# Running the mixer layers on two segments at once, with split norms and streamed mixer weights, in a fused recurrent-attention kernel

## The chip, the cores and the metric

One core of a Trainium2 chip. The metric is the device time of one execution in microseconds (us), lower is better; each figure is a median of several executions. All runs told here are of the undisturbed ("fast") state.

## The reference

Four layers on one sequence of 2048 tokens of width 640: A, B, A, B, each on the layer norm of its input and added to it. Reduced to what matters:

```python
def A(x):                         # x: 2048 x 640, seg 32, 32 heads of 192
    mem = mem0                    # 8 x 640
    for s in range(64):
        h = concat(mem, x[32*s : 32*s+32])          # 40 x 640
        q, k, v = h @ Wq, h @ Wk, h @ Wv            # each 640 -> 6144
        o = softmax(mask(q k^T / sqrt(192))) v @ Wo  # 6144 -> 640
        mem = o[:8]                                  # recurrent
        out[32*s : 32*s+32] = o[8:]

def B(x):
    n = layernorm(x)
    h = gelu(n @ w1)              # 640 -> 640; its quarters are shifted by
    x1 = x + shifted(h) @ w2      # -1, +1, -2, +2 tokens
    return x1 + gelu(layernorm(x1) @ w3) @ w4       # 640 -> 1536 -> 640

x = x + A(layernorm(x)); x = x + B(layernorm(x))    # and the same once more
```

The memory makes A a chain of 64 steps; a step has only 40 rows, but needs all of Wq, Wk, Wv and Wo, 31 MB in bf16, more than fits on the chip.

## The kernel before

Both A layers run in one loop. Iteration t works on segment t of the first A and on segment t - D_LAG of the second ("lanes"), 80 columns together. The heads go in eight groups of four. The weights of A are cut into 64 halves of 480 KB: 26 stay resident, 38 are streamed in each iteration through a ring of six buffers (`wst`) on the queue of SP. Layer B of the segments that A has just finished is cut into stages, one of which is issued at the end of each head group ("fillers"). Rows pass between layers through DRAM: `x1d` (after the first A), `x2d` (after the first B), `x3d` (after the second A).

```python
def a_main(t, hT, hT_n, pc, prep_next, fillers=()):
    cx = a_begin(t, hT, hT_n, pc)
    st_proj(cx, 0)                              # q, k, v of group 0
    if pending_xnew:
        a_xnew(pending_xnew.pop(0))             # x + A, stores to x1d and x3d (SP)
    pc_next = prep_next()                       # a_prep_load: loads of xs (SP) and their norms
    for g in range(NG):                         # NG = 8
        st_scores(cx, g)                        # pss
        if g + 1 < NG: st_proj(cx, g + 1)
        st_softmax(cx, g)                       # mx, nb (VectorE), exp (ScalarE), Pm
        if g >= 1: st_pt(cx, g - 1)             # transposes pst, eviction PT on ScalarE
        if g >= 2: st_wo(cx, g - 2)             # psy += Wo x oT
        if g >= 1: st_pv(cx, g - 1)             # pso, eviction oT on VectorE
        fillers[g]()                            # one stage of layer B
        ...

def s1a():                                      # layer B, first stage; 72 rows of two lanes
    ...
    nc.sync.dma_start(out=xw[...], in_=src[...])    # x1d / x3d
    layer_norm(xw, u, slice(0, XW))             # norm of x, then layer B's own norm of it:
    layer_norm(u, bv_c, slice(0, XW))           # bn_stats x2, bn_aggr, +eps (VectorE),
                                                # pow (GpSimd), apply (VectorE)
...
stages = [s1a, s1b, s1c, s2a, s2b, s2c(0, 6), s2c(6, 6), s3]   # s3 stores x2d and the output (SP)
```

An eviction here is the copy of a matmul's result from a PSUM tile to an SBUF tile. In the trace of this kernel VectorE reaches the eviction of oT only at 2038.65 us, behind the norms that it began at 2032.03. Likewise SP stands 3.74 us (from 2028.12) at the load of xs from `x2d`, until the store of x3d ahead of it has landed.

## Time and profile before

| | before |
|---|---|
| median of 6 runs | 4865.28 us (4852.06 to 4867.98) |
| TensorE busy, granted clock | 4025.0 us (83%), 0.917 |
| VectorE, ScalarE busy | 2805.0 us, 1994.9 us |
| DMA | 1355.8 MB, mean 279 GB/s |
| start, loop, end | 157 us to the second iteration, then 66 iterations of 69.2 us, 141 us from the last start to the end |

"Busy" is an average over the whole run. Where TensorE is busy 83% of the time, the question is what ends its idle time. The granted clock is the share of TensorE's full clock: in a stretch where it was 0.55, fifteen matmuls took 1.21 us instead of 0.70. The prediction shows the lines. In them PE is TensorE, PEld its weight loads, DVE VectorE, ACT ScalarE, POOL GpSimd, SP SyncE; a q behind a name is the engine's own sequencer, which issues DMAs; L297 is a line of the kernel. A line of waits reads: who waited for whom, us in total, times, longest. A row of windows reads: from:to and length in us, busy time (and instructions) of TensorE, weight loads, VectorE, ScalarE, GpSimd, then granted clock, DMA share, GB/s.

### The profile page before, as it was taken

The numbers are of one execution on the slowest core, as the hardware profiler recorded it, in microseconds if no ns is written. First come the engines' busy times: TensorE is split into PE (matmuls) and PEld (weight loads), VectorE is DVE, ScalarE is ACT, GpSimd is POOL, SyncE is SP. The second block draws the span as 40 slices with busy tenths as digits, with TensorE's granted clock in tenths as the row PEclk, the third lists the DMA queues.
The fourth block names the chain that finished last, engine by engine and source line by source line (L and its number), as shares of the span: only waits on it lengthen the run. The fifth ranks groups of instructions, "written<-read, shape, count | busy, mean of one in ns | idle before, by whom it ended". The sixth has DMA issues, their size and how long they took to land.

```text
span 4865.7 us, 174526 instructions
## 1 busy us (share of the span) xinstructions
PE 4025.0 (83%) x74804; PEld 3514.6 (72%) x74804; DVE 2805.0 (58%) x7270; ACT 1994.9 (41%) x7281; POOL 509.0 (10%) x1489
## 2 busy tenths in 40 slices
PE   1898888888988888889888888888889888988886
PEld 1777777777777777777777777777777777777774
DVE  1556555556565556555556565656565655555554
ACT  0444344434444444344434443444344434444442
POOL 1111110111011101110111011101110111011110
PEclk9999999999999999999999999999999999989997
DMA  9888778778887788778778887878788777877882
GB/s 370 306 289 287 267 282 284 281 267 286 292 282 271 281 285 283 266 276 284 279 260 290 283 284 271 285 278 285 269 286 291 280 266 281 293 274 274 287 293 98
DMA packets 437102, 1355.84 MB, mean 279 GB/s; under 512 B 51004, under 2 KB 91972, under 8 KB 436324
## 3 DMA queue, kind: packets, MB, share of 16 engines
q1 hardware_dynamic: 412724, 1320.43, 76.9%
q10 hardware_dynamic: 22368, 18.68, 1.1%
q8 instruction: 584, 9.57, 0.8%
q0 software_dynamic: 1232, 5.57, 0.3%
q14 instruction: 194, 1.59, 0.1%
HBM read 1326.13 MB, written 37.03 MB: 280 GB/s over the span
## 4 chain that ended last, share of the span: by engine, by line
PE 64%; DVE 16%; DMA 12%; POOL 3%; issue 3%; ACT 2%; SPq 0%; DVEq 0%; POOLq 0%; ACTq 0%
PE psv L441 13%; PE psy L548 10%; PE psq L403 10%; PE psk L403 9%; DMA xs<-in_A_x_dram 6%; DVE ln_st L293 5%; PE y2A L719 4%; POOL ln_rstd L296 3%; PE pss L483 3%; DMA wst<-wS 3%; PE hsA L684 3%; PE psh L709 2%; DVE oT L282 2%; PE pso L527 2%; PE pso L532 1%
## 5 line engine op out<-in xcount | busy, mean ns | idle before, releaser
L403 PEld LDWEIGHTS <-wst 128*128 128x128 bf16 x19380 | 824.4, 104 | 55.0 <-issue 28.4
L497 ACT ACTIVATE Pm<-pss,nb 80x80 bf16<-80x80 f32 x2176 | 679.4, 319 | 284.0 <-DVE nb L492 278.9
L441 PEld LDWEIGHTS <-hT 128*80 128x80 bf16 x5440 | 594.9, 119 | 247.4 <-DMA wst<-wS 44.0
L280 ACT CAST V<-psv 80x384 bf16<-80x384 f32 x1088 | 504.4, 477 | 426.6 <-PE psv L441 415.0
L441 PE MATMUL psv<-wst,hT 128*80 128x384 bf16 x3060 | 598.4, 330 | 25.9 <-DMA wst<-wS 21.5
L282 DVE CAST oT<-pso 128x480 bf16<-128x480 f32 x544 | 357.4, 657 | 396.5 <-PE pso L532 392.2
L548 PE MATMUL psy<-oT,wo 128*128 128x80 bf16 x6120 | 316.4, 211 | 294.3 <-DVE oT L282 288.0
L282 DVE CAST kT<-psk 128x480 bf16<-128x480 f32 x544 | 354.2, 651 | 335.7 <-PE psk L403 335.3
L548 PEld LDWEIGHTS <-wo 128*128 128x128 bf16 x6120 | 280.6, 106 | 317.1 <-issue 317.1
L403 PE MATMUL psk<-hT,wst 128*128 128x80 bf16 x10200 | 489.8, 207 | 18.8 <-DMA wst<-wS 17.3
L280 ACT CAST qT<-psq 128x480 bf16<-128x480 f32 x544 | 299.8, 551 | 445.0 <-PE psq L403 444.9
L465 POOL COPY Vz<-V 80x128 bf16<-80x128 bf16 x544 | 157.7, 290 | 3093.9 <-ACT V L280 3093.8
L403 PE MATMUL psq<-hT,wst 128*128 128x80 bf16 x9180 | 452.3, 209 | 20.9 <-ACT hT L367 18.5
L441 PE MATMUL psv<-wv,hT 128*80 128x384 bf16 x2380 | 466.5, 327 | 0.1
L548 PE MATMUL psy<-oT,wst 128*128 128x80 bf16 x10200 | 458.9, 202 | 8.5 <-DMA wst<-wS 7.6
L497 ACT ACTIVATION_READ_ACCUMULATOR Pm<-pss,nb 80x1 f32 x2176 | 428.1, 197 | 0.0
L548 PEld LDWEIGHTS <-wst 128*128 128x128 bf16 x10200 | 402.1, 100 | 11.8 <-DMA wst<-wS 9.7
L403 PE MATMUL psq<-hT,wq 128*128 128x80 bf16 x7140 | 369.2, 211 | 0.0
L282 DVE CAST kTz<-psk 64x160 bf16<-64x160 f32 x1088 | 344.3, 316 | 8.7
L403 PEld LDWEIGHTS <-wq 128*128 128x128 bf16 x7140 | 330.5, 106 | 0.1
L490 DVE TENSOR_REDUCE mx<-pss 80x1 f32<-80x320 f32 x544 | 261.3, 480 | 118.7 <-PE pss L483 110.4
L296 POOL TENSOR_TENSOR ln_rstd<-ln_rstd,neghalf 32x1 f32<-32x1 f32 (+2 forms) x335 | 195.2, 583 | 1113.1 <-DVE ln_rstd L295 738.7
(104 smaller groups left out, 6388.6 us busy)
## 6 DMA issues: line engine op xcount, KB each, us to landing
wst<-wS SPq DMA_DIRECT2D x2584, 480.0 KB
x1d<-xs SPq DMA_DIRECT2D x64, 80.0 KB
xs<-x2d SPq DMA_DIRECT2D x64, 80.0 KB
x3d<-xs SPq DMA_DIRECT2D x64, 80.0 KB
xw<-x1d SPq DMA_DIRECT2D x63, 80.0 KB
x2d<-xw SPq DMA_DIRECT2D x63, 80.0 KB
xw<-x3d SPq DMA_DIRECT2D x63, 80.0 KB
wS<-in_A_Wk_dram ACTq DMA_DIRECT2D x10, 480.0 KB
```

The source lines that it names most:

```text
L280: nc.scalar.copy(out=out_ap, in_=in_ap)
L282: nc.vector.tensor_copy(out=out_ap, in_=in_ap)
L293: nc.vector.bn_stats(out=st[rs, c, :], in_=srcv[:, c, :])
L296: nc.gpsimd.tensor_tensor(out=rstd[rs, :], in0=rstd[rs, :], in1=neghalf[rs, :], op=ALU.pow)
L403: nc.tensor.matmul(out=psq[:, c, :], lhsT=w[:, kc, cc * P:(cc + 1) * P], rhs=hT[:, kc, :], start=(kc == 0), stop=(kc == KC - 1))
L441: nc.tensor.matmul(out=psv[:], lhsT=hT[:, kc, :], rhs=wv[:, kc, :], start=(kc == 0), stop=(kc == KC - 1))
L465: nc.gpsimd.tensor_copy(out=vz[:, :, 0, 0:64], in_=V3[:, SS, 0:64])
L483: nc.tensor.matmul(out=o_, lhsT=l_, rhs=r_, start=False, stop=(n == len(ops) - 1))
L490: nc.vector.reduce_max(out=mx[:], in_=pss[:].rearrange("p h k -> p (h k)"), axis=AX.X)
L497: nc.scalar.activation(out=E[:, i, :], in_=pss[:, i, :], func=ACT.Exp, bias=nb[:], scale=scale, accum_out=sums[:, i:i + 1])
L548: nc.tensor.matmul(out=cx.psy[:, m, :], lhsT=wo[:, cc, m * P:(m + 1) * P], rhs=oT[:, c, :], start=False, stop=last)
L719: nc.tensor.matmul(out=y2A[:], lhsT=h2T[:, c, :], rhs=w4_sb[:, c, 0:512], start=(c == 0), stop=(c == FC - 1))
```

## The change

Intent: do layer B for two segments (128 rows of two lanes instead of 64) in every second iteration, so that its norms, evictions and stages come half as often, and take the norms apart so that no long block of them stands in VectorE's order. Its parts:

- Layer B on pairs of segments, its stages spread over the sixteen head groups of two iterations; the lag grows from 4 to 6, so A runs 70 iterations instead of 68.
- Layer B's weights are streamed (`wB` to `wstB`, a ring of four) once in two iterations; the room goes to 32 resident halves of A instead of 26.
- Norms split into `ln_stats` and `ln_apply`, issued in different head groups, in layer A's preparation too.
- The loads of xs are issued before the first projection, with three buffers.
- Residents are loaded at their first use.
- The rows of layer B (`xw`) are loaded on ScalarE's queue instead of SP's.

```diff
-D_LAG = 4
+B2X = 1
+D_LAG = 6 if B2X else 4
-N_RES_HALVES = 26
+N_RES_HALVES = 32 if B2X else 26
+B_LOAD_Q = "act"
+LAZY_RES = 1
+PT_EARLY = 0
+LN_SPLIT = 1
 ... (cut)
+    def ln_stats(src, rs, key):        # bn_stats, bn_aggr, +eps, pow
+    def ln_apply(h, dst):              # (src - mean) * rstd
 ... (cut)
     def a_main(t, hT, hT_n, pc, prep_next, fillers=()):
+        pc_next = prep_next() if prep_next is not None else None
         st_proj(cx, 0)
-        pc_next = prep_next() if prep_next is not None else None
 ... (cut)
+            if g == 0 and pc_next is not None:
+                a_prep_stats(pc_next)
+            if g == 1 and pc_next is not None:
+                a_prep_apply(pc_next)
             if g < len(fillers) and fillers[g] is not None:
                 fillers[g]()
 ... (cut)
+        def sA():
+            xw = work.tile([XB, Dm], f32, name="xw", bufs=1)
+                {"sp": nc.sync, "act": nc.scalar, "pool": nc.gpsimd}[B_LOAD_Q].dma_start(
+                    out=xw[2 * j0 + Lb:2 * j1:2, :], in_=src[t0_ + j0:t0_ + j1, :])
+            st.h1 = ln_stats(xw, slice(0, XB), "b1")
+        def sA2():
+            ln_apply(st.h1, st.u)
+            st.h2 = ln_stats(st.u, slice(0, XB), "b2")
+        def sA3():
+            ln_apply(st.h2, bv_c)
 ... (cut)
+        stages = [sA, sA2, sA3] ... [sB, sC, sC, sD, sD2, sE, sF, sF, sF, sF, sG]
```

(In the last lines, arguments and the four-row tile `xl_c`, which gets the same norms, are cut.)

## The prediction

> **What bounds the kernel now.** I read the page first (busy shares, then the chain of waits), then the stretch of one iteration on TensorE in order of time, then the waits of TensorE and of the SP queue, then windows. The main loop runs 68 iterations of about 69.2 us (start to start of the one matmul that opens each); ahead of it lie 88 us of loading, behind it 75 us of layer B alone.
>
> The page says that no engine is full, and gives TensorE 64% of the chain:
>
> ```profile
> PE 4025.0 (83%) x74804; PEld 3514.6 (72%) x74804; DVE 2805.0 (58%) x7270; ACT 1994.9 (41%) x7281; POOL 509.0 (10%) x1489
> PE 64%; DVE 16%; DMA 12%; POOL 3%; issue 3%; ACT 2%; SPq 0%; DVEq 0%; POOLq 0%; ACTq 0%
> ```
>
> TensorE's order of time shows where one iteration loses. The reader is to see two holes, 3.92 and 4.12 us, and that fifteen matmuls take 1.16 to 1.21 us after them but 0.70 us later:
>
> ```profile
> 2035.13 0.31 PE L532 MATMUL pso<-PT,Vz 80*128 80x80 bf16 x4
> 2039.36 1.16 PE L548 MATMUL psy<-oT,wo 128*128 128x80 bf16 x15 [3.92 <-DVE oT L282]
> 2044.64 0.48 PE L660 MATMUL psvT<-ident,bv_c 72*128 72x72 bf16 x5 [4.12 <-DVE bv_c L298]
> ...
> 2045.72 1.21 PE L403 MATMUL psq<-hT,wq 128*128 128x80 bf16 x15
> ```
>
> The waits of TensorE show that this happens in every iteration, and that weights still arriving are no cause:
>
> ```profile
> PE psy L548 <- DVE oT L282: 288.0, 134, 4.7
> PE psvT L660 <- DVE bv_c L298: 281.6, 69, 10.4
> ...
> PE psv L441 <- DMA wst<-wS: 21.5, 28, 3.2
> ```
>
> The windows give the clock: 9.65 us with holes, 6.36 us at 0.55 of the clock, then 39.49 us nearly without a gap. The last row is DMA at its fullest, 402 GB/s:
>
> ```profile
> 2034.99:2044.64 9.65, 1.60 (x24) 1.31 (x23) 7.36 (x20) 0.00 (x0) 2.15 (x5) 0.59 0.83 313
> 2044.64:2051.00 6.36, 6.36 (x78) 5.86 (x79) 2.32 (x7) 2.24 (x10) 0.00 (x0) 0.55 0.30 83
> 2051.00:2090.49 39.49, 38.38 (x767) 33.57 (x764) 23.43 (x61) 19.37 (x71) 3.17 (x11) 1.00 0.87 306
> 2070.00:2080.00 10.00, 10.00 (x209) 9.04 (x207) 6.06 (x16) 6.06 (x22) 0.96 (x4) 1.00 1.02 402
> ```
>
> So an iteration is about 55 us of TensorE work at full clock; 8.0 us of two holes; about 3.1 us of half clock (half of 6.36); about 3 us of small waits. The holes come from VectorE: four layer norms stand in one block (L293 to L298), and the eviction of oT and the input of psvT stand behind them. They in turn begin late because the load of xs is issued behind the stores of the residual.
>
> **What the Trainium skill says.** (1) "TensorE: Matmul & The Clock Gate", section "Back-to-back issue gap": isolated matmuls start every N/2.4 + 2.5 ns when warm; it warns that with a weight load each, N=128 sustains about 81 ns. The trace agrees with the formula and not with the warning: thirty 80-column matmuls, each with its own 128x128 weights, take 1.07 us on the chain, 35.7 ns each (formula 35.8); thirty 64-column ones take 0.88 us, 29.3 ns (formula 29.2). (2) The same page, "Part 1: The HAM clock gate": an idle window of about 3.4 us halves the clock. The trace agrees: 3.92 us of idling, then 0.59. (3) "DMA: Bandwidth & Descriptors", section "Bandwidth": a fabric ceiling of 435 GB/s. The trace reaches 402 over 10 us and 361 and 385 over the first two 50 us; stretches with every DMA engine busy average 365 to 374 (an estimate of mine from the packets' times). (4) Same page, "Queues, rings and completion order": SP and ACT have a ring each, consumed in order. The trace shows the store of x3d, behind weights on SP, landing after 5.1 us (issued 2026.8, next load released 2031.9); in the tail, without traffic, store and load together need 4.35 us. Whether the ACT ring is quicker no run here shows.
>
> **The change part by part.**
>
> *Layer B on two segments at once.* w1 and w3 are stationary and the tokens move, so 85 matmuls of 64 columns (29.2 ns) become 85 of 128 (55.8 ns) half as often: 4.96 us a pair becomes 4.74, nothing. In w2 and w4 the tokens are stationary (72 columns of weights, now 128) and 640 columns move: 20 chunks x 0.27 us = 5.4 us each iteration become 5.4 us each second one, saving 2.7 us. Transposes save nothing much. Over the build's matmuls by N/2.4 + 2.5: 3710 us before, 3624 us after. That is 86 us, although two iterations are added: the lag grows from 4 to 6, so 70 iterations instead of 68, about 46.5 us of layer A each (93 us, inside the 3624). The intended arithmetic gain is thus under 2%.
>
> *Norms split and spread.* Statistics and application are issued in different head groups, each layer B norm runs each second iteration, and the loads of xs are issued before the first projection. The order of VectorE in the changed build shows the block gone: evictions of kT and oT stand between its parts. This should remove both holes and the cold clock: 8.0 + 3.1 = 11 us of each iteration. It is the large term. VectorE falls from about 41 to an estimated 38 us an iteration: layer B's norms and adds (8.6 us) are halved, the two chains on the four-row tile add 3.8 us a pair, and GELU stays about 4 us.
>
> *Weights.* 32 instead of 26 halves are resident, paid for by streaming layer B's weights: 32 x 0.4915 MB = 15.73 MB an iteration, plus 6.06 MB a pair, plus about 0.57 MB of rows: 19.33 MB, against 18.68 + 0.57 = 19.25 before. The same bytes must pass in less time. At 52 us an iteration that is 372 GB/s, at 57.5 it is 336. DMA therefore becomes a second wall right behind TensorE.
>
> *A new wait.* After the last stage of a pair, x2d is stored, SP waits for the landing, and loads the rows back for the next prep; the order of VectorE has the statistics of these rows ahead of the next kT eviction. Counted from the end of the last y2 matmul: add 1.3, store about 4, load about 3.5, norm about 2.5: kT is evicted at about 11.7 and its padded copies at 12.3 us, where TensorE wants it at about 9.7. A hole of 2.6 us a pair. At the end of the first iteration of a pair oT stands behind the w2 result and its statistics: another 1.8 us. While SP waits for these stores it issues only some 8 weight loads in 16 us, so the other 94 us of a pair must carry 34.6 MB, 369 GB/s: at the saturated rate.
>
> *Sum.* Pair: 103.6 us of matmuls (3624/70 x 2), 2.6 + 1.8 new holes, 2.6 of the small waits that stay, = 110.6, or 55.3 an iteration. For DMA, which is at its limit with ten buffers to even out the bursts, I add 4% by judgement: 57.5. Start: ACT relays 15.7 MB instead of 18.7 and the residents load during the first iteration; about 55 MB must pass by its end, 147 us at 375 GB/s, so 150 (before: 156.6). Then 69 x 57.5 = 3968. Tail: two passes of layer B of 37 us before; with twice the columns in w1 and w3, partly at half clock, and more GELU calls, 42 each, 85. Total 150 + 3968 + 85 = 4203; I say 4190.
>
> **The rivals.**
>
> *A: DMA alone becomes the bound.* For it: the demand above; windows at 1.02 share. Against it: the 39.49 us stretch at 306 GB/s has a DMA share of only 0.87, and TensorE hardly waits there. If the saturated rate in practice is 340 GB/s, an iteration takes 57 to 58 us; at 315, 61 us and 4450 in all.
>
> *B: the holes move rather than vanish.* The chain store, load, norm, kT takes their place, the hole passes 3.4 us, and the half clock returns. For it: in-order VectorE, and ACT now issues loads that wait for stores, so that evictions stand behind it. Against it: once in two iterations, not each. With a 6 us hole and 3 us of cold clock a pair: 60 us an iteration, 4375.
>
> *C: only the arithmetic counts and the holes are not removed.* Two more iterations against 2.7 us an iteration: about 4780, within 2%. Against it: the order of VectorE.
>
> *D: all goes well*, 53.5 us an iteration: 150 + 3690 + 85 = 3925.
>
> **Range and chances.** Between D and A/B with margins: 3980 to 4430. To stay within 2% (over 4768) an iteration would have to take 65.7 us, that is, most of the 11 us would have to come back. Faster 0.95, within 2% 0.035, slower 0.015.
>
> **What would show it.** TensorE's waits for psvT and for psy behind oT fall from 570 us to under 200 us; its granted clock rises from 0.917 to over 0.96; iterations of 56 to 59 us; mean DMA rate 325 to 345 GB/s with a share over 0.9; waits of psq, psk, psv and psy for wst or of the layer B matmuls for wstB rise from under 60 us in all to some hundreds; a hole of 2 to 4 us before scores once a pair; ACT waiting for the stores of x1d. I am wrong if the clock stays near 0.92 (B or C), if the wait for weights exceeds 400 us (A), or if the start or tail differ by over 40 us from the above.

## The result, and the profile after

| | before | after |
|---|---|---|
| median | 4864.42 us (16 runs) | 4336.24 us (8 runs, 4328.4 to 4339.16) |
| ratio | 1 | 0.8911 (95%: 0.89 to 0.8923) |
| TensorE busy, clock | 4025.0 us, 0.917 | 3823.3 us, 0.964 |
| DMA | 1355.8 MB, 279 GB/s | 1404.7 MB, 324 GB/s |
| start, loop, end | 157 us, 66 x 69.2 us, 141 us | 149 us, 68 x 59.35 us, 145 us |

A ratio here is the mean time of one kernel's fast runs over that of the other's fast runs of the same rounds, so it is not quite the ratio of the medians quoted. The change is 10.9% faster.

The page of the kernel after, busy time and share of each engine with its count of instructions. TensorE is now busy 88%; VectorE's work fell by 153 us although there are two more iterations:

```profile
PE 3823.3 (88%) x72420; PEld 3395.7 (78%) x72420; DVE 2651.7 (61%) x7089; ACT 1992.3 (46%) x7427; POOL 570.8 (13%) x1578
```

TensorE's waits after: psy behind oT fell from 288.0 to 46.7 us, psvT behind the norms from 281.6 to 11.5, and streamed weights are hardly a wait. What leads now is PT, an eviction on ScalarE, which was 63.5 us before:

```profile
PE pso L657 <- ACT PT L369: 161.8, 116, 2.7
...
PE psy L678 <- DVE oT L371: 46.7, 70, 0.7
...
PE psvT L995 <- DVE bv_c L406: 11.5, 1, 11.5
...
PE psv L571 <- DMA wst<-wS: 2.5, 5, 0.6
```

Windows over one iteration before, then over the two of a pair after. The clock goes from 0.90 to 1.00 and 0.97, VectorE from 41.31 us to 38:

```profile
2020.83:2090.49 69.66, 59.50 (x1099) 51.99 (x1098) 41.31 (x107) 29.25 (x108) 7.15 (x21) 0.90 0.79 279
```

```profile
2053.40:2111.90 58.50, 54.67 (x1058) 48.44 (x1056) 38.78 (x101) 29.53 (x108) 7.25 (x20) 1.00 0.96 354
2111.90:2171.30 59.40, 53.03 (x1019) 47.28 (x1016) 37.22 (x103) 27.18 (x104) 8.15 (x23) 0.97 0.89 306
```

TensorE in order of time in that pair (start, length, matmul, the idle time before it and what ended it): the holes of 3.92 and 4.12 us are gone, fifteen matmuls take 0.70 us, and the largest hole left waits for PT in the second iteration of the pair:

```profile
2054.79 0.70 PE L678 MATMUL psy<-oT,wst 128*128 128x80 bf16 x15 [1.04 <-DVE lnrs_b L400]
...
2139.16 0.30 PE L657 MATMUL pso<-PT,V 80*128 80x80 bf16 x4 [2.40 <-ACT PT L369]
```

### An account of one iteration

To compare kernels I split the distance between two starts of TensorE matmuls, as the trace records them, over 52 iterations in the middle of each run. For each matmul the distance to the next is expected to be N/2.4 + 2.5 ns (which the prediction checked against the trace); "matmuls" is the sum of those. Of what exceeds it, pieces over 150 ns are "gaps" and the remainder is "rest", which I take to be mostly half clock. The labels are those of the experiments below. "Change" is the ratio to the kernel before, less one.

| kernel | median us | change | iteration | matmuls | gaps | rest |
|---|---|---|---|---|---|---|
| before | 4864.42 | | 69.45 | 54.43 | 12.34 | 2.68 |
| after | 4336.24 | -10.9% | 59.46 | 51.64 | 6.46 | 1.35 |
| before_early_load | 4800.91 | -1.3% | 68.28 | 54.43 | 11.08 | 2.77 |
| unbatched_prep_split | 4811.94 | -1.0% | 68.57 | 54.43 | 11.53 | 2.62 |
| unbatched_all_split | 4627.80 | -4.8% | 65.69 | 54.43 | 9.92 | 1.35 |
| unbatched_act_loads | 4575.86 | -6.0% | 64.56 | 54.43 | 9.59 | 0.55 |
| unbatched_all_split_lag6 | 4906.52 | +0.9% | 68.88 | 54.43 | 11.97 | 2.49 |
| batched_norms_whole | 4692.03 | -3.5% | 65.08 | 51.64 | 9.85 | 3.59 |
| more_stream | 4720.55 | -2.9% | 64.93 | 51.64 | 11.08 | 2.21 |
| b_weights_once | 4323.26 | -11.1% | 59.26 | 51.43 | 6.79 | 1.04 |
| late_rows | 4422.05 | -9.0% | 60.90 | 51.64 | 7.81 | 1.46 |
| late_rows_pt_early | 4378.71 | -10.0% | 60.30 | 51.43 | 7.93 | 0.94 |
| pt_early | 4267.81 | -12.2% | 58.31 | 51.64 | 5.60 | 1.07 |
| load_q_sp | 4180.45 | -14.1% | 56.99 | 51.43 | 5.31 | 0.26 |

(51.43 against 51.64 for the same matmuls is records missing from a trace, not work saved; the 0.21 us lie in the gaps there.) Of the 10.0 us that an iteration lost from before to after, 2.8 are arithmetic, 5.9 are gaps and 1.3 rest. The two additional iterations give back about 2 x 59.5 = 119 us.

### The profile page after: what moved, and what is told of

It is laid out like the page before. It is cut to its first block, busy times and chain, and to the rows that moved or that the text cites.

```text
span 4329.6 us, 169527 instructions
## 1 busy us (share of the span) xinstructions
PE 3823.3 (88%) x72420; PEld 3395.7 (78%) x72420; DVE 2651.7 (61%) x7089; ACT 1992.3 (46%) x7427; POOL 570.8 (13%) x1578
## 5 line engine op out<-in xcount | busy, mean ns | idle before, releaser
L533 PEld LDWEIGHTS <-wst 128*128 128x128 bf16 x16800 | 727.2, 102 | 32.5 <-issue 28.5
L571 PE MATMUL psv<-wv,hT 128*80 128x384 bf16 x2800 | 547.4, 326 | 1.3 <-DMA wv<-in_A_Wv_dram 1.3
L678 PE MATMUL psy<-oT,wst 128*128 128x80 bf16 x8400 | 396.6, 201 | 108.5 <-DVE lnrs_b L400 60.2
L678 PEld LDWEIGHTS <-wst 128*128 128x128 bf16 x8400 | 348.6, 99 | 131.2 <-issue 129.9
L533 PE MATMUL psq<-hT,wst 128*128 128x80 bf16 x8400 | 409.0, 205 | 21.7 <-ACT hT L497 17.9
L533 PE MATMUL psq<-hT,wq 128*128 128x80 bf16 x8400 | 413.9, 207 | 2.2 <-DMA wq<-in_A_Wq_dram 2.2
L533 PE MATMUL psk<-hT,wst 128*128 128x80 bf16 x8400 | 412.5, 206 | 2.7 <-DMA wst<-wS 2.7
L533 PE MATMUL psk<-hT,wk 128*128 128x80 bf16 x8400 | 407.3, 205 | 2.4 <-DMA wk<-in_A_Wk_dram 2.4
L678 PE MATMUL psy<-oT,wo 128*128 128x80 bf16 x8400 | 399.7, 202 | 0.8 <-DMA wo<-in_A_Wo_dram 0.6
L369 ACT COPY PT<-pst 80x320 bf16<-80x320 bf16 x560 | 242.6, 433 | 277.2 <-PE pst L645 270.5
L533 PEld LDWEIGHTS <-wk 128*128 128x128 bf16 x8400 | 349.8, 102 | 2.8 <-DMA wk<-in_A_Wk_dram 2.7
```

Of the source, the lines that this page charges most:

```text
L369: nc.scalar.copy(out=out_ap, in_=in_ap)
L533: nc.tensor.matmul(out=psq[:, c, :], lhsT=w[:, kc, cc * P:(cc + 1) * P], rhs=hT[:, kc, :], start=(kc == 0), stop=(kc == KC - 1))
L571: nc.tensor.matmul(out=psv[:], lhsT=hT[:, kc, :], rhs=wv[:, kc, :], start=(kc == 0), stop=(kc == KC - 1))
L678: nc.tensor.matmul(out=cx.psy[:, m, :], lhsT=wo[:, cc, m * P:(m + 1) * P], rhs=oT[:, c, :], start=False, stop=last)
```

## The experiments

All kernels passed the comparison with the reference. That comparison is blunt for layer B: b_weights_once, whose layer B multiplies by zeros, passed it too. It says little about layer B's matmuls in any of these kernels.

The first theory (theory 1) was that the gain is the norms taken apart: VectorE's block of them made both holes. Its rivals: batching does it, since everything of layer B then comes half as often (rival 2); or issuing the loads of xs early does (rival 3). Of DMA the prediction had said that it is a second wall (theory A).

### 1. The early load alone, in the kernel before

```diff
-N_RES_HALVES = 26    # xs0, xs1 with the pool's number of buffers
+N_RES_HALVES = 25    # xs0, xs1 with bufs=3; the half makes room
+        pc_next = prep_next()             # loads of xs ahead of the stores
         st_proj(cx, 0)
         a_xnew(pending_xnew.pop(0))
-        pc_next = prep_next()
```

> The kernel before, with only the loads of the next rows issued ahead of the first projection (three buffers for them, and for their room 25 instead of 26 resident halves: one more 480 KB load an iteration). Theory 1 (the holes come from four norms in one block on VectorE): the block starts some 5 us earlier but stays whole, holes shrink by about half, 4700 us. Rival 2 (working on two segments at once, so half as many norm chains, is what removed the holes): no change, 4850 to 4900. Rival 3 (the late load of the rows alone made the holes): nearly the whole gain, about 4450.

Measured 4800.91 us, ratio 0.9874 (0.9855 to 0.9893). TensorE's waits show what happened: the wait for oT fell from 288.0 to 74.6 us and that for psvT from 281.6 to 183.5, but a new one, for streamed weights, took most of it:

```profile
PE psvT L660 <- DVE bv_c L298: 183.5, 69, 10.6
PE psv L441 <- DMA wst<-wS: 122.6, 65, 4.1
...
PE psy L548 <- DVE oT L282: 74.6, 126, 0.7
```

It lies between what theory 1 and rival 2 expected, and rival 3 falls as the explanation of 10.9%: the early load takes away half of the two old waits but is worth 1.3% by itself. One resident half fewer is part of that. What is left is telling: behind the early load psvT, which waits for layer B's two norms, keeps most of its wait, and oT, which stood behind layer A's two, does not.

### 2 and 3. The split of the norms alone, without batching

Layer B on one segment, lag 4, 25 resident halves as in experiment 1; first with layer A's norms alone split, then with layer B's too, in as many stages as before (some old stages merged to make room).

```diff
-B2X = 1          LAZY_RES = 1    HS_SEQ = 1
+B2X = 0          LAZY_RES = 0    HS_SEQ = 0    N_RES_HALVES = 25
 # the second kernel, in addition:
-stages = [s1a, s1b, s1c, s2a, s2b, s2c(0, 6), s2c(6, 6), s3]
+stages = [s1a, s1a2, s1a3, s1bc, s2a, s2ab, s2cc, s3]   # stats | apply + stats | apply | ...
```

> The changed kernel with layer B on one segment as before (lag 4, 68 iterations, weights of layer B resident, 25 resident halves): loads early and the two norms of layer A split, the three norms of layer B still whole. Theory 1: the block is shortened to the two norms of layer B, holes of about 3 us an iteration stay, 4550 us. Rival 2: 4750 or more. Rival 3: the same as before_early_load.

> As unbatched_prep_split, and layer B's norms split over head groups too. Theory 1: iterations of 54.4 us of matmuls plus the 7.8 us of waits and slow clock that the changed kernel has, 62.2 us, so 4460 us: three quarters of the gain without batching. Rival 2: 4700 or more. The part that batching alone brings is then 2.7 us an iteration less two iterations.

Measured 4811.94 us (0.9896, 0.9877 to 0.9915) and 4627.80 us (0.9518, 0.9499 to 0.9538). Theory 1 misses both: the first is what rivals 2 and 3 had expected (splitting A's norms adds nothing to experiment 1), the second lies between theory 1 and rival 2 (splitting all of them, with the early loads, gives less than half of the gain). The clock is nevertheless 0.975, higher than after: the long holes are gone. What remains are waits for weights and many small ones:

```profile
PE psv L571 <- DMA wst<-wS: 110.4, 74, 3.0
PE pso L657 <- ACT PT L369: 85.7, 107, 2.0
...
PE pss L613 <- DVE kT L371: 72.9, 118, 1.9
```

Why weights, at a mean rate of 303 GB/s in mid-run, well below what the kernel after moves? SP's queue in order of time (start, duration of the run of issues, transfer). The store of x2d is issued at 2052.56, and until 2067.54 only six loads of weights follow (two of them in the lines left out); then 26 go in 35 us:

```profile
2052.56 0.47 SPq L935 DMA_DIRECT2D x2d<-xw  x1
...
2055.20 3.76 SPq L359 DMA_DIRECT2D wst<-wS  x4
...
2067.54 35.39 SPq L359 DMA_DIRECT2D wst<-wS  x26
```

SP's own waits say what it stood at: for the results to be stored, of layer B and of A, 591 us in all, in nearly every iteration:

```profile
SPq L935 <- DVE xw L927: 304.5, 61, 5.8
...
SPq L705 <- DVE xs L704: 286.8, 64, 5.5
```

In the kernel after the same waits at the store of x1d are 133.3 us, and the one at the store of x2d comes half as often. That is one thing that batching does. That these stops alone make the weights late isn't shown: the kernel before has them too (266.0 us at the store of x2d, 223.2 at the load behind the store of x3d) and waits 46 us for weights in all, and experiment 6 speaks against it.

### 4. Batching alone: norms in one piece

```diff
-LN_SPLIT = 1
+LN_SPLIT = 0
```

> The changed kernel with every norm whole again (the switch that splits them off), batching kept. Theory 1: holes and half clock come back, at least in every second iteration, 4550 to 4650 us. Rival 2 and rival 3: within 2% of the changed kernel, 4330 to 4400.

Measured 4692.03 us, 0.9646 (0.9628 to 0.9665), clock 0.921. The rivals, in which batching carries nearly everything, fall; theory 1's own figure is missed by 1 to 3%. The wait behind oT is back; those behind kT and the four-row tile are new with batching:

```profile
PE psy L678 <- DVE oT L371: 221.1, 188, 3.5
PE pss L613 <- DVE kT L371: 129.3, 34, 7.9
PE psl L998 <- DVE xl_c L387: 94.0, 35, 3.8
```

So an iteration wins 3.8 us by the split alone (experiment 3), 4.4 us by batching alone, and 10.0 us by both. Neither theory 1 nor rival 2 stands by itself. (Both have the early loads too.) The sum falls short by 1.9 us; experiments 6 and 12 come back to it.

### 5. A longer lag without batching

After experiment 3 it was possible that the unbatched kernel is held by the way from the store of x2d to its reload (theory 1b). A lag of 6, as the changed kernel has, gives that way two iterations more.

```diff
-D_LAG = 4       # unbatched_all_split
+D_LAG = 6
```

> unbatched_all_split with lag 6 instead of 4, so that the rows of x2d that a prep loads were stored two iterations earlier; two iterations more. Theory 1b: the store and reload of x2d in every iteration holds up the SP queue and the statistics on VectorE, and its iterations fall from 65.7 to 61 to 63 us (waits for wst and for kT go), in all 4430 to 4520 in spite of two more iterations. Rival: those waits come from something else (one weight more to stream, or VectorE's load); iterations stay at 65 to 66 us and the total rises by 130 us to 4760.

Measured 4906.52 us, 1.0091 (1.0072 to 1.011): slower by 6% than with a lag of 4, where two iterations of 65.7 us are 2.8%. Theory 1b falls. The rest of the loss is longer iterations, by 3.2 us in mid-run and 2.2 over the whole loop. SP's wait at the store of x2d went from 304.5 to 515.7 us and TensorE's for weights from 110.4 to 171.5, in line with a queue that stands still at its stores; why it stands longer I haven't found, so this run speaks against 1b and for nothing.

### 6. The rows on ScalarE's queue, without batching

If SP's standing still costs weights, moving the loads of the rows (which wait for the stores of x1d and x3d) off SP should help (theory 1c).

```diff
-                nc.sync.dma_start(out=xw[...], in_=src[...])      # unbatched_all_split
+                nc.scalar.dma_start(out=xw[...], in_=src[...])
```

> unbatched_all_split with the loads of layer B's rows on ScalarE's queue, as the changed kernel has them. Theory 1c: in unbatched_all_split the SP queue, which alone issues the weights, stands some 12 us of each iteration at stores that wait for VectorE and loads that wait for those stores; one of the three stops goes, waits for wst fall from 2.5 us an iteration to under 1, and the time from 4628 to 4500 to 4570. Rival: ScalarE then stands at these loads instead (once an iteration, not once a pair) and holds up its evictions: 4600 to 4700.

Measured 4575.86 us, 0.9404 (0.9382 to 0.9426), 1.2% below experiment 3 and 6 us above what 1c expected. TensorE's waits for streamed weights fell from 160 to 72 us in all; that for PT, on ScalarE, has nearly doubled:

```profile
PE pso L657 <- ACT PT L369: 158.1, 116, 2.0
...
PE psk L533 <- DMA wst<-wS: 52.0, 74, 2.9
```

SP's waits at the two stores did not change (306.4 and 284.7 us, 591 as before), so they are not what the other 88 us came from. Its waits for the stores of x1d and x3d at the row loads were only 24 us in experiment 3; what left SP's order is the loads themselves, which in the pair shown there lie for 2.5 us between two loads of weights (2065.1 to 2067.5). Why that costs so much isn't shown.

The changed kernel has its rows on ScalarE's queue too, and so has the batched kernel of experiment 4. With the queue alike, split (4.9 us) and batching (4.4) make 9.3 of the 10.0 us. But this sum counts the queue in both parts, and in the changed kernel the queue has the opposite sign (experiment 12). Batching with whole norms and the rows on SP wasn't run, so how much of the 10.0 us is interplay stays open.

### 7. and 8. Is DMA what sets the pace?

More bytes, then fewer. In the second kernel layer B multiplies by a tile of zeros that is never loaded; its result is wrong.

```diff
-N_RES_HALVES = 32      # more_stream: six more halves streamed in each iteration
+N_RES_HALVES = 26
 # b_weights_once
-            t = wringB.tile([P, HSZ], bf16, name="wstB")
-            nc.sync.dma_start(out=t[:, 0:used], in_=wB[i][:, 0:used])
-            return bp_view(t, nm, a_, b_)
+            return bp_view(zt, nm, a_, b_)
```

> The changed kernel with 26 instead of 32 resident halves: 2.95 MB more an iteration, 22.3 MB instead of 19.3. Theory A (DMA is a wall right behind TensorE, saturated at 365 to 374 GB/s): iterations of at least 60 to 61 us for DMA alone, with the bursts 62 to 64 us, 4520 to 4620, waits for wst of hundreds of us. Rival (DMA has slack, the busy share of 0.9 is mostly queueing): 4330 to 4380.

> The changed kernel without the streaming of layer B's weights: every one of its matmuls reads one zeroed tile (the result is wrong on purpose, the matmuls are the same in number and size). 217 MB of 1405 MB fall away. If DMA does not set the pace of the changed kernel (theory from its waits: 10 us of TensorE's waits in all name a weight load in the loop): 4290 to 4340, the few us from start and tail. If DMA does (theory A): 4200 or less.

More bytes: 4720.55 us, 0.9708 (0.9693 to 0.9723), slower than any theory had said, and its waits are for weights:

```profile
PE psq L533 <- DMA wst<-wS: 168.6, 117, 3.7
...
PE psv L571 <- DMA wst<-wS: 81.7, 86, 35.4
```

Fewer bytes: 4323.26 us, 0.8889 (0.887 to 0.8907), against 0.8911 for the changed kernel: the intervals overlap. The run is less clean than that sounds. A new hole came with it, at kT behind the rows of layer B (first the kernel after, then b_weights_once, where VectorE's wait for the rows rose from 144.4 us):

```profile
PE pss L613 <- DVE kT L371: 23.1, 11, 7.5
```

```profile
PE pss L611 <- DVE kT L369: 125.9, 35, 7.7
DVE ln_st L396 <- DMA xw<-x3d: 232.2, 33, 11.1
```

The wait for PT fell at the same time, from 161.8 to 92.7 us, so what fewer bytes alone are worth can't be read from the total. What speaks against theory A is that TensorE waits 11 us for streamed weights in the whole run, and that the same bytes pass in 4180 us in experiment 12. Where the wall is stays open: with 22.3 MB an iteration (19.33 of the prediction and six halves) more_stream moves 343 GB/s and waits 368 us for weights; load_q_sp moves 339 (19.33 MB in 56.99 us) and waits 33. A limit of the rate just above that, and a ring of six too short for 38 loads an iteration, weren't told apart. Either way the six resident halves, paid for by streaming layer B once a pair, are a needed part of the change: without them the kernel takes 8.9% longer.

### 9 to 11. PT earlier, and the rows later

The leading wait after is PT. Three attempts: transpose and evict P one step earlier (PT_EARLY, an option in the changed kernel); begin layer B one head group later and take the statistics of its rows a group after their load; both.

```diff
-PT_EARLY = 0             # pt_early: st_pt(g - 1) right behind st_scores(g), before st_proj(g + 1)
+PT_EARLY = 1
 # late_rows
-stages = [sA, sA2, sA3, sB, sC, sC, sD, sD2, sE, sF, sF, sF, sF, sG]
+stages = [none, sA, sA1, sA2, sA3, sB, sC+sC, sD, sD2, sE, sF, sF, sF+sF, sG]   # sA1: the statistics
```

> The changed kernel, with the transposes of the probabilities (pst) issued one place earlier, ahead of the next projection, so that ScalarE's copy PT has 4 us instead of 1 us before the product with V. If TensorE's largest remaining wait (pso for PT, 162 us in all) is a plain loss on the path, about 100 to 160 us go: 4180 to 4240. If VectorE or ScalarE behind it set the pace, the wait only moves (to pst for Pm, or to psq for the eviction of qT): 4300 to 4360.

> The changed kernel with layer B's stages moved one head group later and the statistics of its rows a further one after their load, so that neither ScalarE's queue nor VectorE waits for the stores of x1d and x3d and the reload. If the trip through DRAM (2.3 us of ScalarE, 4 us of VectorE a pair) causes most of the late PT copies: 2 to 3 us a pair less, 4240 to 4290. If not: within 0.5% of 4336.

> pt_early and late_rows together. In pt_early TensorE's one large hole left is 5.7 us a pair, at the transposes of Pm, with VectorE ahead of it waiting for the reloaded rows; late_rows takes that wait away and its own loss (late PT copies) is what pt_early cures. If both readings hold: 34 pairs x 5 us less than pt_early's 4268, so 4080 to 4150. Rival: the two changes only move the order of VectorE and ScalarE about; 4260 to 4420.

pt_early: 4267.81 us, 0.8777 (0.8763 to 0.879), 1.5% faster than the changed kernel, between what was expected for and against. The wait of pso for PT is gone from the leading ones, and one of pst for Pm of VectorE came, 143.9 us, mostly in a single hole a pair:

```profile
2106.38 0.46 PE L645 MATMUL pst<-ident,Pm 80*80 80x80 bf16 x4 [5.73 <-DVE Pm L635]
```

late_rows: 4422.05 us, 0.9097 (0.9084 to 0.9111), a miss: slower by 2%. With both, 4378.71 us, 0.8996 (0.8976 to 0.9015), within the rival's range. The trace of late_rows shows that the edit didn't do what I had meant. The load of xw still followed the store of x3d by 4 us and VectorE still stood, 4.17 us in the pair I looked at, at the statistics: its wait for xw was 153.5 us in the whole run, 144.4 in the changed kernel. A stage moved in the program isn't a load moved in time. The wait stayed; that the merged stages make the loss is likely, but not shown.

### 12. One word: the queue of the rows

That left two suspects for late PT: VectorE standing at the rows' statistics, and ScalarE standing in line at the load of the rows. Both hang on the same load.

```diff
-B_LOAD_Q = "act"
+B_LOAD_Q = "sp"
```

> The changed kernel with one word altered: the rows of layer B (tile xw) are loaded on the SP queue, with the weights and the stores, instead of on ScalarE's queue. Theory 1 (what the separate queue buys is that the SP queue isn't held up at the stores, as the pair of unbatched kernels showed with 1.2%): batched, the rows come half as often, so about half of that is lost, 4350 to 4390 us, and TensorE's waits for wst come back with 40 to 150 us. Rival (ScalarE standing in line at the load of xw, some 2.3 us a pair, is what makes PT late in the changed kernel): TensorE's waits of pso for PT fall from 161.8 to under 110 us and the time falls to 4290 to 4325 us. If both happen, the time stays within 4325 to 4350 us.

Measured 4180.45 us (4173.42 to 4189.47), 0.8595 (0.8583 to 0.8607), clock 0.984: 3.5% below the changed kernel's ratio, the fastest of all. Theory 1 of that text falls; its rival had the right direction and expected no more than a third of the size. The same edit had helped the other way round in the unbatched kernel. The traces tell why, and this is the most instructive reading of the study. First ScalarE in the changed kernel: V is evicted at 2122.36, then ScalarE has nothing to do for 2.82 us. The profile names PE psk as the releaser of the next eviction; but just ahead of it ScalarE's queue issues the load of xw, at 2125.16. In the trace it stands at that load's semaphores from 2122.4 on, that is, until the stores of x1d and x3d land (the one of x3d took 5.0 us from its issue in this pair):

```profile
2122.36 0.47 ACT L369 CAST V<-psv 80x384 bf16<-80x384 f32 x1
2125.16 0.46 ACTq L967 DMA_DIRECT2D xw<-x1d  x1
2125.66 0.48 ACT L369 CAST V<-psv 80x384 bf16<-80x384 f32 x1 [2.82 <-PE psk L533]
```

This is no odd pair: the median idle time around that load is 2.1 us, 69 us over the run. While ScalarE stands, SP runs on. Of the nine loads of weights merged in the second line, four are issued ahead of the load of the rows, two more by 2126.51, and three from 2130.72 on:

```profile
2120.26 0.32 SPq L708 DMA_DIRECT2D x3d<-xs  x1
2120.99 14.08 SPq L359 DMA_DIRECT2D wst<-wS  x9
```

The rows travel beside the first six or behind them and land late. VectorE stands 4.03 us at their statistics, with the eviction of oT and the next nb (at 2136.47) behind it; ScalarE's exps wait 4.55 us for that nb, and PT, behind the exps in ScalarE's order at 2138.67, is the 2.40 us hole of TensorE at 2139.16:

```profile
2132.39 0.49 DVE L398 BATCH_NORM_STATS2 ln_st<-xw 128x6 f32<-128x320 f32 x1 [4.03 <-DMA xw<-x3d]
```

With the rows on SP, SP itself waits for the stores. It has issued one load of weights between, not four (so in all 29 pairs counted; in the kernel after the median is four):

```profile
2046.42 0.32 SPq L708 DMA_DIRECT2D x3d<-xs  x1
2046.83 0.37 SPq L359 DMA_DIRECT2D wst<-wS  x1
2049.75 0.48 SPq L967 DMA_DIRECT2D xw<-x1d  x1
```

and VectorE finds the rows there:

```profile
2053.84 0.89 DVE L398 BATCH_NORM_STATS2 ln_st<-xw 128x6 f32<-128x320 f32 x2
```

From issue to landing the rows of x1d take 6.2 us on ScalarE's queue and 2.5 us on SP's (medians of the two pages). Over the whole run VectorE's wait for xw<-x3d fell from 144.4 us to 28.3 (first the kernel after, then load_q_sp), TensorE's for PT from 161.8 to 99.6:

```profile
DVE ln_st L398 <- DMA xw<-x3d: 144.4, 33, 8.4
```

```profile
DVE ln_st L398 <- DMA xw<-x3d: 28.3, 21, 5.3
PE pso L657 <- ACT PT L369: 99.6, 128, 2.2
...
PE psk L533 <- DMA wst<-wS: 13.5, 15, 2.0
```

The waits of psk and psv for weights rose to 26 us only (13.5 and 12.8): SP's standing for three microseconds once a pair costs TensorE little. In the unbatched kernel the row loads came in each iteration, and taking them off SP helped. In the account, gaps fell by 1.15 us an iteration and rest by 1.09: nearly half of the gain is the clock. The traces' records of the granted clock show it: in the 52 iterations the kernel after has 32 stretches at half clock, 150 us in all, and 31 holes of TensorE over 2 us; load_q_sp has no such stretch and no hole over 1.97 us. The run doesn't tell how much of the 3.5% is the earlier rows and how much ScalarE not standing; one edit did both.

pt_early and load_q_sp together weren't run. What remains of pt_early's hole might be the same rows (VectorE waits 128.3 us for xw<-x3d there), but that is only argued.

## Why the prediction was right or wrong

It said 4190 us (its own sum gives 4203), and 4336 came, inside the range of 3980 to 4430; iterations of 59.35 us lie just above the 56 to 59 that it named. Its steps:

- **Both holes vanish with the norms' block, and the clock comes back.** Right: the two waits fell from 570 to 58 us, the clock rose to 0.964 (over 0.96 was predicted). But it credited that to the split and gave batching under 2%. Experiments 3 and 4 show that this is where the reasoning was thin: the split without batching makes 4.8%, batching without the split 3.5%. In the unbatched kernel the split removes the long holes and waits for weights grow instead (46 to 160 us); in the batched one the whole norms still block. "Four layer norms stand in one block" was also read too coarsely: in the trace layer A's two norms (2032.03 to 2038.62, with the eviction of kT and other work between) stand ahead of oT, and layer B's two (2039.34 to 2044.58) behind it, ahead of psvT. Experiment 1 bears that out: loading layer A's rows early took 213 of the 288 us at oT, but 98 of the 282 at psvT.
- **Arithmetic.** Right: 51.8 us an iteration against 51.64.
- **Start 150, end 85.** Right: the second iteration begins at 148.7 us, and layer B alone takes 86 us at the end.
- **DMA, 4% on each iteration, "by judgement".** This term of the sum wasn't there: 2.2 us of 57.5. Waits for streamed weights are 11 us in the whole run where "some hundreds" were expected, and experiment 12 passes the same bytes in 4180 us. Rival A falls with it. Six halves more do make TensorE wait (experiment 7), whatever the limit there is. The mean rate of 324 GB/s lies just beside the 325 to 345 predicted.
- **New holes and small waits, 7.0 us a pair, with the clock whole.** This is the term that was mis-sized: gaps are 6.46 us an iteration, or 12.9 a pair, and 1.35 us an iteration of rest comes on top. Part of the miss lies in the sum: the prediction counts "about 3 us of small waits" an iteration before, but carries 2.6 a pair, less than half, without a reason. In the trace, gaps under 1 us are 3.58 us an iteration before and 3.10 after, that is 6.2 a pair: they stayed. The larger gaps are 6.7 a pair, where 4.4 were worked out. The hole that was worked out, from the store of x2d over its reload to kT, hardly exists: pss waits for kT 23.1 us in the whole run. VectorE's order was read rightly, but its neighbour wasn't sized: the rows of layer B on ScalarE's queue. Rival B had named it, "ACT now issues loads that wait for stores, so that evictions stand behind it", with 60 us an iteration and 4375 us. That is closer to what came (59.46 us, 4336 us) than the point figure, though of B's main chain, a 6 us hole at kT and then half clock, only the half clock came: the hole is at PT, 2.40 us in the pair shown. Experiment 12 moves the rows off ScalarE's queue and 156 us go, about as much as the point figure missed by. That both land near 4190 is partly chance, since the DMA term was wrong in the other direction.
- **The clock whole.** Not so: of the 32 stretches at half clock in the 52 iterations of the account (2.9 us an iteration), all but one had no hole over 2.70 us just before. The prediction counted on half clock only after about 3.4 us of idling, its point (2), and read the trace before as agreeing. That reading was too coarse: there the clock is at half from 2036.72 us on, 1.3 us into the first hole.
- **"Whether the ACT ring is quicker no run here shows."** Experiment 12 shows it for these rows, with weights going out beside them: 6.2 us from issue to landing on ScalarE's queue, 2.5 on SP's.

## What to carry to other kernels

Taking a long block apart removes its holes, but something else can come in their place; split and batching, each with the early loads, were worth 4.8% and 3.5% alone and 10.9% together, with six more resident halves. Try a load that waits for a recent store on the queue that issued the store, if that queue can spare the time: in load_q_sp it held back the bulk loads behind it, and no computing engine stood in line for it. Test it in the kernel as it is, since the same edit had the opposite sign before batching. When a small term of a sum is carried on, carry it at its measured size: small waits stayed at 3 us an iteration. When an engine idles and the profile names a releaser that was done long ago, look at what its own queue issued just before.

## What the Trainium skill lacked or had wrong

- "TensorE: Matmul & The Clock Gate", section "Part 1: The HAM clock gate": it lacks how much idling short of a whole window is enough. In the kernel after TensorE idled for 65% (median; 51% at least) of the 3.41 us ahead of a stretch at half clock, and the longest hole among it was 2.66 us (median).
- "TensorE: Matmul & The Clock Gate", section "Back-to-back issue gap": it gives a sustained 81 ns a matmul at N=128 where each has its own weight load. The kernel after runs its 128-column matmuls, each with its own 128x128 weights, every 56 ns (median over 2828 distances between starts of layer B's psh), which is the page's formula for isolated ones.
- "DMA: Bandwidth & Descriptors", section "Issuing engines are not separate DMA queues": it says that DMAs of different engines share the 16 DMA engines, and that issuing from several saves only sequencer time, "usually small relative to the DMA itself". The first fits what the runs show. It lacks that the choice can cost: with the rows on ScalarE's queue they landed 6.2 us after issue instead of 2.5, ScalarE idled 2.1 us a pair around the load (median), and the kernel took 4336 us instead of 4180.
- No page that I read has the price of an issuing queue that stands in order at a store. These runs don't give it either: in the kernel with split norms and no batching SP waited 591 us at stores and TensorE 160 us for streamed weights, at a mean rate of 303 GB/s; with the rows' loads moved to ScalarE's queue the 591 us stayed and the 160 became 72.
- "DMA: Bandwidth & Descriptors", section "Bandwidth": its table has 341 GB/s for a transfer of 1 MB and 425 for one of 16 MB, and lacks the rate of many smaller loads in flight at once. With loads of 480 KB through a ring of six, stores and rows between, load_q_sp moved 339 GB/s with 33 us of waits for weights and more_stream 343 with 368; 402 GB/s were seen over 10 us.
